# Hash attention and a gated block: the sums of a pair moved half a pair later, and for late pairs put beside the hash products of the next

## The chip, the cores and the metric

The kernel runs on one core of a Trainium2 chip. Times are device microseconds (us) of one launch; the kernel before was run three times. One further execution was recorded by the profiler. TensorE (PE) multiplies matrices into PSUM, ScalarE (ACT) applies functions, VectorE (DVE) does elementwise work, GpSimd (POOL) and SyncE (SP) here mainly issue DMAs. [...]

## What is computed

Attention in which a query sees only the keys of its own hash bucket, and then a gated feed-forward block on the result:

```python
q_bits = (np.einsum('bhsd,dk->bhsk', q, proj) > 0)      # 6 bits per token, k likewise
mask = q_bucket[:, :, :, None] == k_bucket[:, :, None, :]
scores = np.where(mask, scale * q @ k.T, -1e9)
attn = softmax(scores)                                   # over keys
x = (attn @ v)                                           # to (B*S, H*D)
g = x @ w_gate
out = (silu(g) * (x @ w_val)) @ w_out
```

There are 4 batches, 8 heads, 768 tokens and 64 channels a head; the block has 3072 tokens, width 512 and inner width 1536. The weights arrive as 8-byte numbers and are split on the chip into float32 parts ("words", "stage").

## The kernel before

The attention stage works on 16 pairs of heads (4 in each batch, NP = 4), and each pair n has two halves of 384 query tokens ("rows" of the work in the change's name). A half runs in three steps, written out by hand in the loop at lines 535 to 570; the order of that code is the order of each engine's queue.

First come six chunks of scores (`score`, 433): for both heads a float32 product of q and k and a bf16 product of hash bits into two PSUM banks, and then two exponentials on ScalarE (446) into the ring of A tiles. `add` (470) sums the A tiles of the half on VectorE (475, 479), one instruction per chunk from the second on, into `acc`, of which there are three. Last come six chunks of value products (`attend`, 449), which accumulate in the single av bank; at their end ScalarE copies av to xT (468), and in half 0 it also writes the small tile e (467), allocated at 466 from the pool `small`, which has two buffers per name.

All other PSUM tiles (scores, sums, hash, transposes) come in turn from one pool of seven banks (235), so that a tile waits until the last reader of the tile seven places before it is done.

Around this, the loop does three pieces of side work:

- **The sums.** `total` (484) multiplies the two acc tiles of a finished pair by a tile of ones (490, a 128x32 stationary operand, four column tiles side by side), ScalarE copies the result to row (493), and a small DMA on SP fetches few (495). `invert` (498) takes reciprocals on VectorE (499), writes them to DRAM (501) and reads them back spread over partitions as r (508, two DMAs). `norm` (512) multiplies xT by r on VectorE (514). For the pairs of the first batch it is followed by `split` (ScalarE 215, VectorE 218 and 222), for the others by a store to DRAM (519).
- **The next pair's operands.** `front` (350) returns steps. Up to pair 4 q and k are transposed by TensorE (356) and copied by ScalarE (359). From pair 5 on ("late") VectorE transposes blocks (410) that eight DMAs have fetched (268). Then `hash_next` multiplies by the hash matrix (369, also 128x32), ScalarE takes the signs of q at once (374), SP copies them to the other partitions (386, qb<-qb), and the rest, the signs of k and their spread on VectorE (383), is kept in the list `rest`, which the loop finishes after the scores.
- **The weights.** `scale_ahead` puts work on ScalarE (132, 124, 125), `prepare_on` on VectorE (150 to 166) and stores on POOL (168, with the loads of 117).

In pair n before the change: half 0 puts the sums of pair n-1 after its second chunk of scores, then the transposes of pair n+1, then `invert`; half 1 puts the hash products of pair n+1 after its third chunk, then the eight raw loads of pair n+2, the rest of the hash after the scores, and norm of pair n-1.

Of the kernel before, what the change touches and what calls it, by code (L numbers as in the profile page):

```python
# [19 lines left out]
def kernel(  # L20
# [29 lines left out]
    NP = H // 2  # L50
# [30 lines left out]
    def finish(todo):  # L81
        while todo:
            todo.pop(0)()
# [12 lines left out]
    n = 0  # L96
# [37 lines left out]
    def scale_ahead():  # L134
        if unrounded:
            round_up()
        i = progress["scaled"]
        if i < NPIECE and i < progress["kept"] + 3 and i in words:
            scale(i)
# [34 lines left out]
    def prepare_on(n):  # L174
        for _ in range(n):
            next(preparing, None)
# [17 lines left out]
    def bring(count=1):  # L194
        for _ in range(count):
            i = len(held)
            if i == len(wanted):
                return
            what, n = wanted[i]
            at = place[what, n % NF]  # L200
            while progress["kept"] <= at:
                next(preparing)
            held[what, n] = t = ringp.tile([P, 3, PIECE], FP32R, tag="ring", name="ring")
            nc.gpsimd.dma_start(t.bitcast(FP32), ram[at].bitcast(FP32))  # L204
# [23 lines left out]
    def attention(scope):  # L228
# [8 lines left out]
        def bank(name):  # L237
            return banks.tile([P, 512], FP32, tag="ps", name=name)
# [34 lines left out]
        def load(n, names):  # L273
            if n < len(pairs):
                for name in names:
                    fetch(n, name, nc.sync)
# [151 lines left out]
        waiting = []  # L428
# [4 lines left out]
        def score(u):  # L433
            n, half, c = units[u]
            qs = slice(half * HQ, (half + 1) * HQ)
            ks = slice(c * P, (c + 1) * P)
            sc = [bank("sc")[:, 0:HQ] for _ in range(2)]
            for x, start in ((T, True), (bits, False)):
                if u < 2 and not start:
                    prepare_pair(1)  # L440
                for h in range(2):
                    rows = slice(h * D, (h + 1) * D)
                    nc.tensor.matmul(sc[h], x["k", n][rows, ks], x["q", n][rows, qs],  # L443
                                     start=start, stop=not start)
            for h in range(2):
                nc.scalar.activation(weights(u)[:, h, 0:HQ], sc[h], AF.Exp,  # L446
                                     scale=SCALE * (OFF / 2 if n <= NP else 1.0))

        def attend(u):
            n, half, c = units[u]  # L450
            a = weights(u)
            if c == 0:
                av[n] = av_ps.tile([P, 512], FP32, tag="av", name="av")
            ps = av[n]
            width = AW if half == 0 else HQ
            for h in range(2):
                nc.tensor.matmul(ps[h * D : (h + 1) * D, 0:width], raws["v", n][:, h, c, :],  # L457
                                 a[:, h, 0:width], start=c == 0, stop=c == NCH - 1)
            if c == NCH - 1:
                if half == 0:  # L460
                    if n == len(pairs) - 1:
                        t = odd_x[NP - 1].tile([P, 3, S], FP32, tag=f"x{NP - 1}", name="lastx")
                        xT[n], spread[n] = t[:, 0], t[:, 1]
                    else:
                        xT[n] = xp.tile([P, S], FP32, tag="xT", name="xT")
                    mean[n] = small.tile([P, 1], FP32, tag="e", name="e")
                    nc.scalar.activation(mean[n], ps[:, HQ : HQ + 1], AF.Copy, scale=EPS)
                nc.scalar.copy(xT[n][:, half * HQ : (half + 1) * HQ], ps[:, 0:HQ])

        def add(u):  # L470
            n, half, c = units[u]
            a = weights(u)
            if c == 1:
                acc[n, half] = att.tile([P, 2, HQ], FP32, tag="acc", name="acc", bufs=3)
                nc.vector.scalar_tensor_tensor(out=acc[n, half], in0=weights(u - 1)[:, :, 0:HQ],
                                               scalar=S * EPS / P, in1=a[:, :, 0:HQ],
                                               op0=ALU.add, op1=ALU.add)
            elif c > 1:
                nc.vector.tensor_tensor(acc[n, half], acc[n, half], a[:, :, 0:HQ], op=ALU.add)  # L479
# [4 lines left out]
        def total(n):  # L484
            ps = bank("sum")
            t = [acc.pop((n, half)) for half in range(2)]
            for h in range(2):
                for half in range(2):
                    g = (2 * h + half) * BLOCK
                    nc.tensor.matmul(ps[g : g + BLOCK, 0:HQ], ones, t[half][:, h, :],  # L490
                                     start=True, stop=True)
            row = att.tile([P, HQ], FP32, tag="row", name="row", bufs=1)
            nc.scalar.copy(row, ps[:, 0:HQ])
            few = small.tile([P, each], FP32, tag="few", name="few")
            nc.sync.dma_start(few, row.rearrange("(g r) t -> r g t", r=BLOCK)[0])
            waiting.append(lambda: invert(n, few))

        def invert(n, few):
            nc.vector.reciprocal(few, few)
            s = sums[n % 2]  # L500
            nc.sync.dma_start(s, few)
            if n == len(pairs) - 1:
                t = spread[n].rearrange("p (x q) -> p x q", x=2)
            else:
                t = att.tile([P, 2, HQ], FP32, tag="r", name="r")
            flat = s.rearrange("p e -> (p e)").rearrange("(h x t) -> h (x t)", h=2, t=HQ)
            for h in range(2):
                nc.sync.dma_start(t[h * D : (h + 1) * D].rearrange("p x t -> p (x t)"),
                                  flat[h : h + 1].to_broadcast([D, 2 * HQ]))
            return lambda: norm(n, t)  # L510
# [13 lines left out]
        rest = []  # L524

        def prepare_pair(count):
            for _ in range(count):
                if steps:
                    rest.extend(f for f in steps.pop(0)() or [] if f)
# [4 lines left out]
        last = []  # L534
        for u in range(0, N, NCH):
            n, half, _ = units[u]
            more = n + 1 < len(pairs)
            for c in range(NCH):
                score(u + c)
                if u + c == 2 or more and half == 1 and c == 2:  # L540
                    prepare_pair(1)
                if half == 1 and c == 2:
                    load(n + 2, "qk")
                if c == 1 and half == 0 and n > 0:
                    total(n - 1)
                if c:
                    add(u + c)
            finish(rest)
            if half == 0 and more:
                steps = front(n + 1)  # L550
                if u:
                    prepare_pair(2)
            if half == 0:
                while waiting:
                    last.append(waiting.pop(0)())
            else:
                finish(last)
            for _ in range(1 if u else 2):
                scale_ahead()
            for c in range(NCH):  # L560
                attend(u + c)
            scale_ahead()
            if half == 1:
                load(n + 2, "v")
            elif more:
                if n + 1 <= NP:
                    prepare_pair(2 if u else 4)
            prepare_on(5 if 0 < n < NP else 4)
            if u >= N - 7 * NCH:
                bring()  # L570
# [5 lines left out]
    with ExitStack() as scope:  # L576
        attention(scope)
# [190 lines left out]
```

## Time and profile before

| | |
|---|---|
| median of 3 runs | 991.44 us (988.75 to 995.03) |
| profiled execution | 989.91 us, span on the core 988.0 us |
| mean granted TensorE clock | 0.981 |
| TensorE matmul busy | 952.0 us, 96% |
| weight loads / VectorE / ScalarE / GpSimd busy | 723.8 / 672.4 / 473.2 / 124.9 us |
| attention stage | 0 to 358 us; the gated block takes the rest |

A page of the profile gives, for each group of instructions, its source line, engine, operation, output and inputs, how many there are, the busy time and mean duration, and the idle time of the engine just before them with what ended it. A timeline lists the same instructions in order of time: start, duration, engine, line, operation, tiles, count, and in brackets the idle time before them and its releaser. Durations overlap where an engine is pipelined, so the distance between starts is what an instruction costs its queue. In the attention stage 2 to 4 such matmuls run side by side.

### The profile page before, as it was taken

Reading aid. Unit: us, or ns where it says so; the run is one execution under the profiler, and the core shown is the slowest. Engines: PE = TensorE matmul, PEld = TensorE weight load, DVE = VectorE, ACT = ScalarE, POOL = GpSimd, SP = SyncE. Lnnn points to the kernel's source line nnn. Section 1 sums busy time; section 2 is a strip of 40 time slices with the busy share of each in tenths; the row PEclk is TensorE's granted clock in tenths of the full one; section 3 lists DMA queues with packets and bytes.
Section 4 is the critical chain, followed back from the end, with each engine's and each line's share of the span. In section 5 each row is a group of like instructions: output and inputs, shape, how many; then the busy total and the mean of one; then the engine's idle time right before and its main releaser. Section 6 shows DMA issues by size and latency. Waiting matters only on the chain.

```text
span 988.0 us, 14458 instructions
## 1 busy us (share of the span) xinstructions
PE 952.0 (96%) x5413; PEld 723.8 (73%) x5413; DVE 672.4 (68%) x868; ACT 473.2 (48%) x882; POOL 124.9 (13%) x248
## 2 busy tenths in 40 slices
PE   9999989999999798788999999999999999999998
PEld 4444434444434368687999999999999999999997
DVE  4788988889877665647886446586546586546556
ACT  6899777887867553333422332322332322232221
POOL 3110010100111012011210110110110110110100
PEclk9999999999999898889999999999999999999999
DMA  6566677788888676485775854655854655754641
GB/s 181 169 184 186 151 175 202 194 210 202 200 207 261 183 264 239 161 298 197 300 280 181 312 191 142 232 207 185 310 189 156 226 205 192 255 189 163 224 160 65
DMA packets 134262, 203.22 MB, mean 206 GB/s; under 512 B 92912, under 2 KB 98512, under 8 KB 134192
## 3 DMA queue, kind: packets, MB, share of 16 engines
q0 software_dynamic: 31008, 159.79, 46.0%
q1 hardware_dynamic: 102384, 42.30, 17.7%
q8 instruction: 43, 0.70, 0.3%
q10 hardware_dynamic: 800, 0.20, 0.1%
q14 instruction: 27, 0.22, 0.1%
HBM read 162.01 MB, written 39.42 MB: 204 GB/s over the span
## 4 chain that ended last, share of the span: by engine, by line
PE 78%; DMA 6%; issue 6%; ACT 4%; DVE 3%; SPq 2%; ACTq 0%; DVEq 0%; POOLq 0%
PE a L597 23%; PE o L597 17%; PE sc L443 13%; PE n L597 12%; PE av L457 10%; DMA qb<-qb 3%; DMA ram<-stage 2%; SPq L268 2%; ACT A L446 2%; PE sum L490 1%; PE hps L369 1%; PE tps L356 1%; DVE o L689 1%; ACT qb L374 1%; DVE acc L479 1%
## 5 line engine op out<-in xcount | busy, mean ns | idle before, releaser
L597 PE MATMUL a<-xparts,ring 128*128 128x384 f32 x1536 | 286.5, 338 | 4.6 <-ACT g L639 3.2
L597 PEld LDWEIGHTS a<-xparts,ring 128*128 128x128 f32 x1536 | 272.0, 190 | 7.4 <-ACT g L639 3.6
L597 PE MATMUL o<-ring,hid 128*128 128x512 f32 x864 | 204.4, 397 | 8.9 <-ACT v L639 5.9
L597 PEld LDWEIGHTS o<-ring,hid 128*128 128x128 f32 x864 | 165.0, 192 | 44.5 <-ACT v L639 6.3
L446 ACT ACTIVATE A<-sc 128x384 f32<-128x384 f32 x384 | 157.7, 510 | 23.3 <-PE sc L443 22.9
L443 PE MATMUL sc<-qT,kT 64*128 64x384 f32 x768 | 166.5, 507 | 0.2 <-ACT A L446 0.2
L597 PE MATMUL n<-xparts,ring 128*128 128x384 f32 x768 | 150.1, 337 | 3.1 <-DVE o L689 3.1
L597 PEld LDWEIGHTS n<-xparts,ring 128*128 128x128 f32 x768 | 135.8, 190 | 3.4 <-DVE o L689 3.4
L479 DVE TENSOR_TENSOR acc<-acc,A 128x768 f32<-128x768 f32 x128 | 122.7, 958 | 22.0 <-ACT A L446 10.2
L645 DVE TENSOR_TENSOR v<-v,n 128x768 f32<-128x768 f32 x48 | 45.8, 954 | 128.4 <-PE n L597 101.7
L457 PE MATMUL av<-A,vraw 128*64 128x386 f32 (+1 forms) x768 | 131.2, 491 | 0.0
L204 POOL DMA_DIRECT2D ring<-ram x144 | 75.9, 529 | 436.8 <-PE n L597 282.5
L443 PEld LDWEIGHTS sc<-qT,kT 64*128 64x128 f32 x768 | 69.5, 189 | 73.0 <-issue 53.7
L457 PEld LDWEIGHTS av<-A,vraw 128*64 128x64 f32 x768 | 52.3, 136 | 71.8 <-issue 59.7
L639 ACT ACTIVATE g<-a 128x768 f32<-128x768 f32 x48 | 38.9, 811 | 126.6 <-PE a L597 126.6
L650 ACT ACTIVATE hid<-v 128x768 fp32r<-128x768 f32 x48 | 40.7, 847 | 115.9 <-DVE v L649 115.9
L689 DVE TENSOR_TENSOR o<-o 128x512 f32<-128x512 f32 x96 | 65.8, 687 | 27.7 <-ACT o L684 25.2
L647 ACT ACTIVATE g<-g 128x768 f32<-128x768 f32 x48 | 40.6, 847 | 87.8 <-DVE g L645 87.8
L443 PE MATMUL sc<-qb,kb 64*128 64x384 bf16 x384 | 69.7, 326 | 7.2 <-DMA qb<-qb 5.8
L645 DVE TENSOR_TENSOR g<-g,n 128x768 f32<-128x768 f32 x48 | 45.6, 949 | 37.8 <-PE n L597 29.7
L168 POOL DMA_DIRECT2D ram<-stage x36 | 19.7, 547 | 379.3 <-ACT A L446 165.2
L653 DVE SCALAR_TENSOR_TENSOR hid<-hid,v 128x768 fp32r<-128x768 f32 x48 | 45.9, 956 | 31.1 <-ACT hid L650 31.1
(77 smaller groups left out, 712.2 us busy)
## 6 DMA issues: line engine op xcount, KB each, us to landing
ring<-ram POOLq DMA_DIRECT2D x144, 768.0 KB, 5.6
ram<-stage POOLq DMA_DIRECT2D x36, 768.0 KB, 4.6
vraw<-in_v_dram SPq DMA_DIRECT2D x16, 384.0 KB
words<-in_moe_w_out_dram POOLq DMA_DIRECT2D x12, 512.0 KB, 7.1
out_dram<-o SPq DMA_DIRECT2D x24, 256.0 KB
r<-sums SPq DMA_DIRECT2D x30, 192.0 KB
words<-in_moe_w_gate_dram POOLq DMA_DIRECT2D x11, 512.0 KB, 7.4
words<-in_moe_w_val_dram POOLq DMA_DIRECT2D x11, 512.0 KB, 7.7
```

Source lines behind the costliest of these rows:

```text
L204: nc.gpsimd.dma_start(t.bitcast(FP32), ram[at].bitcast(FP32))
L443: nc.tensor.matmul(sc[h], x["k", n][rows, ks], x["q", n][rows, qs], start=start, stop=not start)
L446: nc.scalar.activation(weights(u)[:, h, 0:HQ], sc[h], AF.Exp, scale=SCALE * (OFF / 2 if n <= NP else 1.0))
L457: nc.tensor.matmul(ps[h * D : (h + 1) * D, 0:width], raws["v", n][:, h, c, :], a[:, h, 0:width], start=c == 0, stop=c == NCH - 1)
L479: nc.vector.tensor_tensor(acc[n, half], acc[n, half], a[:, :, 0:HQ], op=ALU.add)
L597: nc.tensor.matmul(ps, w, x, start=start, stop=stop)
L639: nc.scalar.activation(two(z), ops[what][2], AF.Copy, scale=STEP + 1)
L645: nc.vector.tensor_tensor(two(z), two(z), n_, op=ALU.subtract)
L647: nc.scalar.activation(z, z, AF.Silu)
L650: nc.scalar.activation(h, val, AF.Copy, scale=TOWARD / STEP)
L653: nc.vector.scalar_tensor_tensor(out=l, in0=h.bitcast(FP32), scalar=-STEP, in1=val, op0=ALU.mult, op1=ALU.add)
L689: nc.vector.tensor_tensor(accs[c], accs[c], t[:, 1], op=ALU.subtract)
```

## The change

The sums of pair n-1 move from the second chunk of half 0 of pair n to the start of half 1, right behind the value products of half 0, for n from 1 to 14; in the last pair they stay. Where pair n+1 is late (n from 4 on), its hash products are issued right behind those sums, ahead of the first scores of half 1, and the rest of the hash is finished after the second chunk of scores. `invert` moves from half 0 to half 1, after its scores, and `norm` from half 1 to half 0 of the following pair, after its transposes. The raw loads keep their place in the loop. The functions called are the same.

```diff
@@ -535,13 +535,21 @@
             n, half, _ = units[u]
             more = n + 1 < len(pairs)
+            final = not more
+            late = n + 1 > NP
+            if half == 1 and n > 0 and not final:
+                total(n - 1)
+            if half == 1 and more and late:
+                prepare_pair(1)
             for c in range(NCH):
                 score(u + c)
-                if u + c == 2 or more and half == 1 and c == 2:
+                if u + c == 2 or more and half == 1 and c == 2 and not late:
                     prepare_pair(1)
+                if half == 1 and c == 1 and late:
+                    finish(rest)
                 if half == 1 and c == 2:
                     load(n + 2, "qk")
-                if c == 1 and half == 0 and n > 0:
+                if c == 1 and half == 0 and final:
                     total(n - 1)
                 if c:
                     add(u + c)
@@ -550,11 +558,13 @@
                 steps = front(n + 1)
                 if u:
                     prepare_pair(2)
-            if half == 0:
-                while waiting:
-                    last.append(waiting.pop(0)())
-            else:
-                finish(last)
+            if half == 1:
+                finish(last)
+            while waiting and (half == 1 or final):
+                last.append(waiting.pop(0)())
+            if half == 0:
+                finish(last[:-1] if final else last)
+                last[:] = last[-1:] if final else []
             for _ in range(1 if u else 2):
                 scale_ahead()
             for c in range(NCH):
```

## The prediction

> **What bounds the kernel now.** I read the page first. TensorE is busy 96% of the span, so what counts is what lengthens its queue. The change touches only the attention stage (0 to 358 us), so I then listed TensorE, ScalarE and VectorE there in order of time. This is pair 11, half 0 from 244.88 and half 1 from 255.11, on TensorE (start, us, engine, line, operation, tile):
>
> ```profile
> 246.86 0.85 PE L490 MATMUL sum<-acc,ones 128*32 128x384 f32 x8
> 247.64 0.92 PE L443 MATMUL sc<-qT,kT 64*128 64x384 f32 x4
> 251.07 4.11 PE L457 MATMUL av<-A,vraw 128*64 128x386 f32 x24
> 255.11 0.92 PE L443 MATMUL sc<-qT,kT 64*128 64x384 f32 x4
> 257.74 0.52 PE L369 MATMUL hps<-qT,hash 128*32 128x384 f32 x2
> 258.52 0.92 PE L443 MATMUL sc<-qT,kT 64*128 64x384 f32 x4
> 261.14 4.09 PE L457 MATMUL av<-A,vraw 128*64 128x384 f32 x24
> ```
>
> There is no gap in it: the pair lasts 20.1 us from sum to sum (246.86 to 266.98). A chunk of scores takes 0.81; a half with neither sums nor hash is 9.07 (348.12 to 357.19: scores 5.05, value products 4.02). A half with either is about 0.98 longer. Eight such matmuls, four at a time, fill 0.64; the other 0.34 are two changes of tile shape, 0.17 each.
>
> The eleven pairs 4 to 14 last from the sums at 98.99 to those at 339.87: 240.9 us. At 20.1 they would be 221.1, so 19.8 are stalls. The list of waits (total, times, longest) names them:
>
> ```profile
> PE sc L443 <- DMA qb<-qb: 5.8, 4, 2.7
> PE hps L369 <- DVE qT L410: 5.4, 2, 5.0
> DVE xT L514 <- DMA r<-sums: 5.2, 3, 2.9
> ACT e L467 <- PE av L457: 14.1, 10, 2.7
> ```
>
> The first two lines are TensorE's. With what follows them (lost clock, the signs' spread) the waits on qb make about 10 of the 19.8; the late raw load of the last pair makes 7.35 (27.46 between sums at 312.41 and 339.87). The last line says that ScalarE is now ahead when it reaches line 467.
>
> The cost of an idle TensorE is in the clock, by stretches of 2 us (length, then busy times, clock, DMA share, GB/s):
>
> ```profile
> 286.00:288.00 2.00, 0.52 (x3) 0.12 (x2) 1.00 (x2) 0.49 (x1) 0.00 (x0) 1.00 1.38 164
> 288.00:290.00 2.00, 1.75 (x11) 0.71 (x14) 1.97 (x4) 0.63 (x2) 0.00 (x0) 0.69 0.78 116
> 290.00:292.00 2.00, 2.00 (x10) 0.51 (x4) 1.66 (x3) 1.21 (x3) 1.78 (x3) 0.50 0.92 173
> ```
>
> 1.73 us of idleness (0.27 and 1.46) was followed by half clock from about 288.75 to 292.16, which cost 1.6 us. Yet 2.71 us at 140.64 to 143.35 cost none. Stepping back from 288.75 by 43 windows of 3.413 us (the figure of the clock page named below), a boundary falls at 141.99 and cuts that gap into 1.35 and 1.36 (1.55 with a 0.20 before it): so between 1.55 and 1.73 idle in one stretch of 3.41 halves the next one.
>
> **The Trainium skill.** "TensorEngine Tiling (Array Packing)", Key Properties: a change of tiling mode drains TensorE; the trace agrees, 0.17 us each. "TensorE: Matmul & The Clock Gate", Part 1: the clock is halved by a monitor with free-running windows of about 3.4 us, after an idle window; the trace agrees on length and phase, but half an idle window was enough. The same page, Architectural detail: ScalarE and VectorE are strict queues, only weight loads are pulled ahead; the lists here show no exception. "PSUM — Partial Sum Buffer", Specifications: eight banks of 2 KiB. This kernel keeps one for av, and seven rotate.
>
> **The change, part by part.** The counts of instructions stay. ScalarE as it runs now in half 1 of pair 11, and VectorE in the last half of pair 15, which has neither sums nor hash:
>
> ```profile
> 255.26 0.17 ACT L467 ACTIVATE e<-av 128x1 f32<-128x1 f32 x1 [1.54 <-PE av L457]
> 255.32 0.47 ACT L468 COPY xT<-av 128x384 f32<-128x384 f32 x1
> 256.28 2.45 ACT L446 ACTIVATE A<-sc 128x384 f32<-128x384 f32 x6 [0.49 <-PE sc L443]
> 258.66 1.16 ACT L374 ACTIVATE qb<-hps,columns 32x384 bf16<-32x384 f32 x2
> 262.27 1.18 ACT L374 ACTIVATE kb<-hps,columns 32x384 bf16<-32x384 f32 x2
> ...
> 351.00 0.96 DVE L475 SCALAR_TENSOR_TENSOR acc<-A 128x768 f32<-128x768 f32 x1 [0.79 <-ACT A L446]
> 352.06 4.14 DVE L479 TENSOR_TENSOR acc<-acc,A 128x768 f32<-128x768 f32 x4
> ```
>
> (1) *TensorE's own work.* Half 0 loses the sums: 9.07. Half 1 has both products in one shape: 9.07 + 1.28 + 0.17 = 10.5. Together 19.6 against 20.1: three changes fewer, 0.5 us saved per late pair, if nothing waits. For pairs 1 to 3 only sums move, one change fewer: under 0.5 us in all; I take zero.
>
> (2) *The bank of the hash.* Seven banks rotate. Half 1 now takes sum, hash, two each for chunks 0 and 1, one for chunk 2; its second goes into sum's bank, and chunk 3 into the hash's bank, which is free only after the two k signs. These stand on ScalarE after chunk 1's exponentials. Before, the hash's bank was next wanted in the following half.
>
> (3) *A wait that moves to ScalarE.* Tile e (line 466, two buffers) is written at the end of half 0 of pair n and reuses the buffer of pair n-2. Its reader is norm, line 514. Before, norm(n-2) ran in half 1 of n-1, long past. Now it runs in half 0 of pair n, on VectorE behind the adds and both transposes. So line 467 waits for it, and behind 467 stand the copies of xT and row, all signs and exponentials of half 1.
>
> Times from the start of the sums in half 1 (t = 0), pairs 6 to 14. VectorE in half 0: adds end 8.0 after its start (348.12 to 356.13, above), transposes 0.89 and 0.94 (253.72, 254.62), norm 1.0: 10.8, which is t = 1.75. The second transpose ends at 0.77, so hash starts at 0.8, not 0.65, and scores at 1.6. ScalarE: e 1.8, xT 1.86, row 2.25, q signs 2.65 and 3.2, then four exponentials of 0.405 to 5.4, k signs of 0.58 to 6.6. TensorE has finished chunk 2 at 4.3 and stands until 6.65: **2.35 us idle**. Then three chunks 2.45 and value products 4.02: half 1 takes 13.1, the pair 13.1 + 9.07 = 22.2, **+2.1 each, 19 for nine pairs**.
>
> Pairs 4 and 5 are worse. Their half 0 normalises pairs 2 and 3, whose split (line 215, ScalarE) follows norm and stands ahead of the weight work (132, 124, 125) and of e. From norm at 10.8: 0.75, then 0.5 + 0.6 + 0.65, e and xT 0.45: row ends its slot at 14.1, t = 5.1 instead of 2.65. Half 1 becomes 15.5, the pair 24.6: +4.5; ScalarE enters pair 4 late from the transposing pairs, about 1.6, and stage work may add as much: I take **13 for both** (9 to 16).
>
> (4) *Clock.* An interval of 2.35 puts 1.65 or more into one 3.41 window for (3.41 - 2.35 + 2 x 0.70)/3.41 = 72% of phases. Loss 1.6 at full overlap; I take 1.2 on average: 9 x 0.72 x 1.2 = 8, and 2 x 1.6 = 3 for pairs 4 and 5, idle over 4: **+11** (0 to 17).
>
> (5) *What is regained.* q signs finish at 3.8 and the DMA of qb is wanted at 14: ten us instead of six (issue 303.87, wanted at 309.9), and r<-sums no longer stands ahead of it on SP. Its longest landing was 7.3, so these stalls go (10). k spread on VectorE also ends before half 0. The eight raw loads follow qb, start some 1.5 us earlier within a longer pair, and are wanted 1.8 earlier: the 7.35 goes mostly. Regained: **19.8** (10 to 19.8).
>
> (6) *SP and POOL.* SP's order becomes few, qb, eight loads, sums, two r, v, xram. r is issued after the loads (5.5 to 17 us of issue) near t = 15.5 and wanted at t = 22.9: 7.4 us, as now (258.26, wanted 265.3). But a late r now stops norm, and so ScalarE, and so TensorE: 0 to 10 us; I take zero, as a rival holds it. v has a whole pair of slack; POOL's order is unchanged. The reciprocal comes later and no longer waits for few (7.7 us of VectorE), hidden behind the adds' own pace.
>
> Sum: 19 + 13 + 11 - 19.8 = +23, less 0.5 for the early pairs: **+22**. Against the profiled execution, 989.91 us, that is 1012; this execution lies 1.5 below the median of 991.44. I keep 1012.
>
> **Rivals.**
> - *Clock holds* (22%): without (4), +11: 1002. For: 2.71 us passed once without loss. Against: the gaps recur at all phases.
> - *r comes late* (19%): three waits of 1.7 in the trace become TensorE's, doubled by loads ahead of them: +10, 1022.
> - *The other side: norm is not late* (13%). If norm ended before t = 0.15, or e's buffer was free otherwise, ScalarE would start row at 0.92 and the k signs would end at 5.8: idle 1.5, below the clock's limit, pair 21.4, eleven pairs 235.4, and 2 of stalls left: 237.4 against 240.9, 986. The point is whether VectorE reaches norm 1.6 us sooner; the adds' pace in the trace speaks against it.
> - *Banks do not bind* (4%): k signs done by 4.3. Pair 19.6, 216 in all, 5 left of the load stall: -20, 970. Against: from 0.9 ScalarE has 0.4 + 1.17 + 1.62 + 1.17 before it, 5.3 at best. This is also the case in which the change does what its words say.
>
> **The numbers.** The forecast itself has 42%. 1% of the median (981.5 to 1001.4) is what a measurement can tell from no change. Faster: the last rival and an edge of the third, 0.05. Within: most of the third and nearly half of the first, 0.21. Slower: 0.74. Range 990 to 1028: it leaves out the last rival, most of the third, and a late r with every clock window lost.
>
> **What would show it.** Gaps of about 2.3 us ahead of the fourth score chunk of half 1, ended by ScalarE's kb sign; line 467 ended by VectorE's 514 in pairs 6 to 14; the waits of PE on qb<-qb gone; granted clock below 1 in the slices from 110 to 340 us; pairs of 22 to 24 us, pairs 4 and 5 longest. I am wrong if chunk 3 follows chunk 2 without a gap, or if VectorE's norm ends before the value products of half 0.

## The result and the profile after

The changed kernel takes 1020.37 us (median of 4 runs, 1017.17 to 1024.35) against 991.24 us for the kernel before in the same comparison: a ratio of 1.0292, 95% interval 1.0242 to 1.0343. Its profiled execution has a span of 1019.5 us, 31.5 more than before, at a mean granted clock of 0.975.

The gated block is not where the time went: from its first product to the end of the span it takes 629.9 us (389.58 to 1019.5), before 629.4 (358.64 to 988.0). The attention stage is 30.9 us longer. TensorE's rows in the page of the kernel after (engine totals, then groups: busy time, mean ns, idle time before them and what ended most of it):

```profile
PE 968.9 (95%) x5413; PEld 737.9 (72%) x5413; DVE 672.5 (66%) x868; ACT 470.4 (46%) x882; POOL 124.9 (12%) x248
...
L443 PE MATMUL sc<-qT,kT 64*128 64x384 f32 x768 | 187.5, 527 | 14.1 <-ACT row L493 7.7
...
L443 PE MATMUL sc<-qb,kb 64*128 64x384 bf16 x384 | 83.4, 336 | 0.6 <-DVE kb L383 0.5
```

The wait of the scores on the DMA of qb is gone (0.6 us of idle time ahead of the second row, none of it the DMA). In its place the first row waits for ScalarE's copy of the row of sums. The list of waits between 90 and 395 us says what ScalarE waits for (engine, line, releaser: total us, times, longest):

```profile
ACT e L467 <- DVE xT L514: 39.7, 7, 10.1
...
DVE kb L383 <- ACT kb L374: 26.5, 11, 2.7
...
DVE xT L514 <- DMA r<-sums: 14.3, 7, 3.0
...
PE hps L369 <- DVE qT L410: 8.0, 2, 7.3
PE sc L443 <- ACT row L493: 7.7, 7, 2.3
```

The first line is the largest change: ScalarE stands at the small tile e until VectorE's norm has read the older one. Before, the same instruction waited only for TensorE's value products. In three more pairs the trace names the hash as the releaser of 467, which doesn't read it; in the one shown below norm ends at 254.65, as the hash does, and e begins at 254.74. So this list has only part of it.

Halves, from the first value product to the next half's first value product, in us ("half 1" of pair n, then half 0 of pair n+1):

| pair | before | after |
|---|---|---|
| 3 | 10.88, 10.36 | 15.61, 9.16 |
| 4 | 10.07, 10.99 | 17.38, 9.06 |
| 5 | 10.60, 13.44 | 15.10, 9.07 |
| 6 | 10.08, 10.05 | 13.71, 9.06 |
| 7, 10, 12 | 10.06 to 10.07, 10.21 to 13.84 | 12.10 to 12.15, 9.06 to 9.07 |
| 8, 9, 11, 13 | 10.07, 10.05 to 11.45 | 14.86 to 15.93, 9.06 to 9.07 |
| 14 | 17.41, 10.05 | 21.81, 10.05 |

Half 0 shrank by one microsecond as it had to; half 1 grew by 2 to 7. Pair 10 is an undisturbed one. TensorE in its half 1 (start, us, engine, line, operation, tiles, count):

```profile
253.00 0.85 PE L490 MATMUL sum<-acc,ones 128*32 128x384 f32 x8
253.81 0.52 PE L369 MATMUL hps<-qT,hash 128*32 128x384 f32 x2
...
257.26 0.97 PE L443 MATMUL sc<-qT,kT 64*128 64x384 f32 x3
...
259.60 1.10 PE L443 MATMUL sc<-qT,kT 64*128 64x384 f32 x3
...
261.11 4.09 PE L457 MATMUL av<-A,vraw 128*64 128x384 f32 x24
```

and ScalarE beside it:

```profile
254.74 0.17 ACT L467 ACTIVATE e<-av 128x1 f32<-128x1 f32 x1 [3.15 <-PE hps L369]
254.81 0.47 ACT L468 COPY xT<-av 128x384 f32<-128x384 f32 x1
255.17 0.50 ACT L493 COPY row<-sum 128x384 f32<-128x384 f32 x1
255.54 1.15 ACT L374 ACTIVATE qb<-hps,columns 32x384 bf16<-32x384 f32 x2
256.72 1.64 ACT L446 ACTIVATE A<-sc 128x384 f32<-128x384 f32 x4
258.38 1.16 ACT L374 ACTIVATE kb<-hps,columns 32x384 bf16<-32x384 f32 x2
```

A chunk takes 0.81, and chunk 2 starts at 256.31, so chunk 3 (257.26) is 0.14 late, right behind the first exponential (256.72 to 257.21): by its start it was given a bank that an exponential frees. The last chunk (259.60) begins 0.06 after the k signs end (259.54), and in v2, v3 and v5 below too it begins 0.04 to 0.05 after them (183.76 after 183.72 in v3): it is taken to be the one in the hash's bank. The half lasts 12.1 us.

Pair 8 is a disturbed one. VectorE's norm there comes late, because r has not landed:

```profile
204.88 0.94 DVE L410 STREAM_TRANSPOSE qT<-qraw 128x768 f32<-128x768 f32 x1
207.64 1.02 DVE L514 SCALAR_TENSOR_TENSOR xT<-xT,e,r 128x768 f32<-128x768 f32 x1 [1.83 <-DMA r<-sums]
```

ScalarE waits for it, with everything of half 1 behind:

```profile
208.76 0.17 ACT L467 ACTIVATE e<-av 128x1 f32<-128x1 f32 x1 [4.96 <-DVE xT L514]
```

TensorE then runs out of banks twice:

```profile
209.74 0.59 PE L443 MATMUL sc<-qT,kT 64*128 64x384 f32 x1 [0.56 <-ACT row L493]
...
211.27 1.31 PE L443 MATMUL sc<-qT,kT 64*128 64x384 f32 x3 [0.47 <-ACT A L446]
```

and the clock follows, in stretches of 2 us (length, busy times of PE, PEld, DVE, ACT, POOL, granted clock, DMA share, GB/s):

```profile
208.00:210.00 2.00, 1.44 (x10) 0.61 (x5) 1.97 (x4) 1.24 (x4) 0.00 (x0) 1.00 0.23 94
210.00:212.00 2.00, 1.53 (x7) 0.76 (x7) 0.93 (x2) 1.96 (x6) 0.86 (x2) 0.94 0.31 109
212.00:214.00 2.00, 2.00 (x10) 1.50 (x9) 0.41 (x1) 1.94 (x5) 0.20 (x1) 0.50 1.01 313
```

One late landing of 1.83 us so makes half 1 14.94 us long instead of 12.1. Norm waits for r (1.43 to 3.04 us) in pairs 6, 8, 9, 11 and 13, the five long ones, and the clock falls to half in three of them (8, 9 and 13).

### The profile page after: what moved, and what is told of

It is laid out like the page before. It is cut to its first block, busy times and chain, and to the rows that moved or that the text cites. A ratio compares the mean times of both kernels' runs of the same rounds, so it can differ in the third digit from the quotient of the medians.

```text
span 1019.5 us, 14489 instructions
## 1 busy us (share of the span) xinstructions
PE 968.9 (95%) x5413; PEld 737.9 (72%) x5413; DVE 672.5 (66%) x868; ACT 470.4 (46%) x882; POOL 124.9 (12%) x248
## 4 chain that ended last, share of the span: by engine, by line
PE 50%; issue 5%; DMA 3%; DVE 2%; ACT 1%; ACTq 0%; POOLq 0%
PE a L607 22%; PE o L607 16%; PE n L607 11%; DMA ram<-stage 3%; DVE o L699 1%; DVE o L696 0%; ACT words L125 0%; ACT stage L124 0%; DVE v L655 0%; DVE hid L663 0%; ACT g L657 0%; ACT v L649 0%; DVE v L659 0%; DVE stage L152 0%; ACT L657 0%
## 5 line engine op out<-in xcount | busy, mean ns | idle before, releaser
L607 PE MATMUL o<-ring,hid 128*128 128x512 f32 x864 | 202.3, 393 | 10.1 <-ACT v L649 5.9
L443 PE MATMUL sc<-qT,kT 64*128 64x384 f32 x768 | 187.5, 527 | 14.1 <-ACT row L493 7.7
L607 PEld LDWEIGHTS o<-ring,hid 128*128 128x128 f32 x864 | 162.7, 189 | 45.8 <-ACT v L649 6.4
L446 ACT ACTIVATE A<-sc 128x384 f32<-128x384 f32 x384 | 155.1, 510 | 9.1 <-PE sc L443 8.5
L443 PEld LDWEIGHTS sc<-qT,kT 64*128 64x128 f32 x768 | 87.3, 198 | 84.2 <-issue 44.2
L443 PE MATMUL sc<-qb,kb 64*128 64x384 bf16 x384 | 83.4, 336 | 0.6 <-DVE kb L383 0.5
L655 DVE TENSOR_TENSOR g<-g,n 128x768 f32<-128x768 f32 x48 | 45.6, 950 | 37.3 <-PE n L607 29.4
```

Source lines behind the costliest of these rows:

```text
L607: nc.tensor.matmul(ps, w, x, start=start, stop=stop)
L655: nc.vector.tensor_tensor(two(z), two(z), n_, op=ALU.subtract)
```

## The experiments

Each kernel below was timed in alternation with the kernel before (990.75 to 992.19 us beside them). Ratios are to that, with the 95% interval.

| kernel | us | ratio |
|---|---|---|
| the change | 1020.4 | 1.0292 (1.0242 to 1.0343) |
| v1: e in four buffers | 1008.5 | 1.0192 (1.0167 to 1.0218) |
| v2: v1, norm in half 1 | 998.5 | 1.0082 (1.0060 to 1.0104) |
| v3: only the hash moved | 1001.7 | 1.0125 (1.0097 to 1.0153) |
| v4: only the sums moved | 1014.7 | 1.0251 (1.0222 to 1.0280) |
| v5: v2, spread later | 995.3 | 1.0038 (1.0015 to 1.0061) |
| v6: v5, norm first | 1000.2 | 1.0087 (1.0043 to 1.0132) |
| v7: v3, spread later | 1002.6 | 1.0112 (1.0087 to 1.0138) |
| v8: v2, hash back in its place | 981.5 | 0.9906 (0.9863 to 0.9950) |
| v9: v6, k signs late again | 988.6 | 0.9975 (0.9961 to 0.9989) |
| v10: v8, hash behind chunk 0 | 982.7 | 0.9918 (0.9888 to 0.9948) |
| v12: the change, k signs late again | 1017.7 | 1.0271 (1.0228 to 1.0313) |
| v13: v9, early hash from pair 6 on | 986.2 | 0.9948 (0.9933 to 0.9963) |

**First question: is it the wait of e, and which half of the change makes it?** The theory was that the reuse of e carries the delay of norm to ScalarE. v1 is the change with

```diff
-                    mean[n] = small.tile([P, 1], FP32, tag="e", name="e")
+                    mean[n] = small.tile([P, 1], FP32, tag="e", name="e", bufs=4)
```

> The changed kernel with four buffers for the tile e instead of two. My theory: line 467's wait for norm (39.7 us of ScalarE in seven waits) is what makes half 1 of pairs 6 to 13 last 12.1 to 15.9 us; without it row is copied near 0.9 us after the sums start, the k signs end near 5.8, and half 1 lasts 10.5 to 10.8. That takes 25 to 28 us off: 1020 becomes 992 to 996. Pairs 4 and 5 (17.4 and 15.1) stay long, because line 215 still waits for norm. Rival, the bank of the hash alone binds: half 1 stays at 12 us or more in pairs 6 to 13 and the time stays above 1008.

Measured 1008.5: 12 us gone, half of what the theory wanted, and neither account holds: the time is on the rival's side of 1008, the halves are not. Line 467 no longer waits for norm, and half 1 of the undisturbed pairs 6, 8, 9 and 11 falls to 11.34 to 11.52 us, not to 10.8. Pairs 4 and 5 stay long (20.44 and 15.30), and VectorE still stands when r is late, with the adds behind norm. That is now VectorE's longest wait:

```profile
DVE xT L514 <- DMA r<-sums: 24.3, 9, 5.6
```

v2 puts norm back into half 1, now of the pair after, where r has had a whole pair:

```diff
-            if half == 0:
+            if half == 0 and final:
                 finish(last[:-1] if final else last)
```

> As the run with four buffers of e, and norm moved from half 0 back to half 1, one half later than in the changed kernel, so that it stands behind the adds of half 1 and r has a whole pair to land. My theory: line 215 no longer waits in half 0, half 1 of pairs 3, 4 and 5 falls from 15.6, 17.4 and 15.1 to about 11, 10.7 and 10.7, and pairs 6 to 13 stay at 10.5 to 10.8: 974 to 982, faster than the kernel before (991). Rival, moving sums and hash costs by itself, whatever norm does: 995 or more.

Measured 998.5: another 10 us, and the rival's range held. With both waits off ScalarE the kernel is still slower than before. v3 and v4 split the change. v3 is the kernel before with these lines alone (`late` as in the change):

```diff
+            if half == 1 and more and late:
+                prepare_pair(1)
...
-                if u + c == 2 or more and half == 1 and c == 2:
+                if u + c == 2 or more and half == 1 and c == 2 and not late:
                     prepare_pair(1)
+                if half == 1 and c == 1 and late:
+                    finish(rest)
```

> The kernel before with the hash products of late pairs alone moved ahead of the first scores of half 1; sums, reciprocals and norm stay where they were. My theory: the waits on qb<-qb go (about 10 us with what follows them), no long gap appears, since line 467 waits for nothing new, and the second transpose delays the hash by about 0.5 us a pair: 980 to 988. Rival, the hash's bank binds: each late pair 1 to 2 us longer, 995 to 1005.

v4 is the change without the moved hash:

```diff
-            late = n + 1 > NP
+            late = False
```

> The changed kernel with the hash products left behind the third chunk of scores in all pairs; sums, reciprocals and norm stand where the change puts them. My theory: line 467 still waits for norm, and behind a late r, so half 1 is long in the same pairs, but the hash's bank no longer adds to it: 1000 to 1012. Rival, the hash's place causes the loss: 991 or below.

Both missed, each on the slow side: the hash alone costs 10.9 us against the kernel before in the same runs (990.8), the sums alone 23.9, together 29.1: less than the sum of both. v3 lies in its rival's range. In its trace half 1 of pair 7 is 1.0 us longer than before: 0.47 is a wait of the hash for the second transpose, and the last chunk, which follows the k signs by 0.04, takes 0.6 more than before (183.76 to 185.28, 1.52 instead of 0.91). Pairs 4, 5 and 14 together are 7 us longer than before. In v4 the wait on norm is larger than in the change itself:

```profile
ACT e L467 <- DVE xT L514: 51.3, 9, 11.4
```

So e and norm belong to the moved sums. The early hash has a cost of its own, which v1 and v2 don't touch.

**Second question: what does the early hash cost?** In v2 an undisturbed pair lasts 21.13 to 21.26 us (pair 11 from value product to value product: 261.52 to 282.65). TensorE's own share, as foretold, would be 19.6, but it waits for VectorE's transpose (0.67 of idle time ahead of the hash at 267.08). VectorE around it:

```profile
266.09 0.93 DVE L410 STREAM_TRANSPOSE qT<-qraw 128x768 f32<-128x768 f32 x1
...
272.05 0.85 DVE L383 TENSOR_SCALAR kb<-kb,columns 32x768 bf16<-32x768 bf16 x2 [2.40 <-ACT kb L374]
272.83 0.94 DVE L475 SCALAR_TENSOR_TENSOR acc<-A 128x768 f32<-128x768 f32 x1
273.87 4.15 DVE L479 TENSOR_TENSOR acc<-acc,A 128x768 f32<-128x768 f32 x4
277.94 1.01 DVE L514 SCALAR_TENSOR_TENSOR xT<-xT,e,r 128x768 f32<-128x768 f32 x1
...
287.35 0.94 DVE L410 STREAM_TRANSPOSE qT<-qraw 128x768 f32<-128x768 f32 x1
```

This reads as a loop, a circle of steps of which each needs the one before it or stands behind it in its queue: transposes, hash (TensorE), q signs, exponentials, k signs (ScalarE), spread, adds, norm, the adds of half 0, transposes (VectorE). Nothing in it is slow, but it is 21.1 us long, and VectorE stands 2.40 us in it. v5 cuts it where the wait stands, by issuing the spread behind the adds of chunks 1 to 3:

```diff
-                if half == 1 and c == 1 and late:
-                    finish(rest)
+                if half == 1 and c == 1 and late and more:
+                    finish([rest.pop(0), rest.pop(0)])
+                if half == 1 and c == 4 and late:
+                    finish(rest)
```

> The run with four e buffers and norm in half 1, and in the late pairs the VectorE step that spreads the k signs (L383) issued behind the adds of chunks 1 to 3 instead of ahead of all adds; the two sign operations on ScalarE stay where they are. Theory A, a loop through VectorE and ScalarE of 21.1 us a pair (the spread stands ahead of the adds and waits for the signs, the transposes stand behind the adds, the next signs behind the transposes): the wait of L383 on ACT kb (30.8 us there) falls under 5 us, the hash's wait on DVE qT goes in most late pairs, a pair lasts 19.6 to 20.2 us, and the kernel takes 983 to 990 us. Theory B, the 21.1 us come from something else (the banks of chunks 3 to 5, ScalarE's order): a pair stays at 21 us and the kernel at 994 to 1001 us.

Theory A fell in this form: 995.3 us is in the rival's range, and an undisturbed pair still takes 21.02 us. VectorE in v5 shows why:

```profile
205.07 0.96 DVE L475 SCALAR_TENSOR_TENSOR acc<-A 128x768 f32<-128x768 f32 x1 [1.59 <-ACT A L446]
207.16 2.02 DVE L479 TENSOR_TENSOR acc<-acc,A 128x768 f32<-128x768 f32 x2 [1.13 <-ACT A L446]
```

The 2.40 us did not go; they are now 1.59 + 1.13 of waiting for exponentials, which stand on ScalarE behind the q signs and behind the k signs. On this reading the loop was not cut, since it also runs through the exponentials. v7 makes the same edit to v3:

> The run that moved only the hash of the late pairs (sums in half 0 as before), and in it the spread of the k signs behind the adds of chunks 1 to 3. Theory A: the wait of L383 on ACT kb (26.1 us there) goes, half 1 goes from 11.1 to about 10.1 us, some 9 us less: 990 to 995 us. Theory B: half 1 stays at 11.1 us because the hash's own products and its bank make it longer: 998 to 1004 us.

1002.6, and half 1 11.03 instead of 11.08 to 11.13 us: the place of the spread decides nothing there either. v6 takes work out of the loop instead, norm into the time in which VectorE waits anyway:

```diff
+            if half == 1 and n > NP:
+                finish(last)
             if half == 1 and n > 0 and not final:
                 total(n - 1)
```

> The run before it in this list, and in the late pairs norm (VectorE, 0.93 us) issued ahead of everything in half 1 instead of behind its scores. Theory A: norm fills time in which VectorE would wait, so the adds of half 0 end 0.9 us earlier; where VectorE still sets the pair this gives another 0 to 8 us, 977 to 988 us. Theory B: the copy of xT that norm reads ends late, so norm waits at the head of VectorE and the adds behind it with it: 990 to 1000 us.

The pairs do what theory A says: half 1 of pairs 6 to 13 is 11.32 to 11.36 us, with no wait for the transposes left, and a pair 20.4. The time does not: 1000.2 us, over a wide spread (994.28 to 1005.24). In the trace, which is of the shortest of its runs, half 1 of pairs 4 and 5 takes 14.59 and 17.38 us, and the last pair gives more back. Its sums run in half 0, so r comes late for a norm at the head of half 1: norm waits 2.60 us for r there, the reciprocal 3.59 for few just before, the adds stand behind both, and the last sums wait 5.26 for them. The trace cannot show why the median is 5 us above v5's: the profiled executions of the two differ by 0.4 us.

What is left of half 1, 11.35 against 10.57 of TensorE's own work, was ascribed to the k signs ahead of the exponentials. v9 is v6 with the early finish taken out and norm first only where another pair follows:

```diff
-                if half == 1 and c == 1 and late and more:
-                    finish([rest.pop(0), rest.pop(0)])
-                if half == 1 and c == 4 and late:
-                    finish(rest)
...
-            if half == 1 and n > NP:
+            if half == 1 and n > NP and more:
```

> The run with four e buffers, norm first in half 1 (not in the last pair, where it waited for r) and the hash ahead of the second row's scores, but the k signs where the kernel before has them, behind all exponentials of half 1, and their spread behind all adds. Theory A, what is left of the cost of the early hash is the two k sign operations ahead of the exponentials of chunks 2 to 5 (half 1 lasts 11.35 us with them, of which TensorE's own work is 10.57): half 1 goes to 10.6 us, a pair to 19.7 us, and the kernel takes 971 to 979 us, less than the run that left the hash in its place (981.5). Theory B, the hash's bank is then held through half 1 and the scores of chunks 3 to 5 wait for banks: half 1 stays at 11.2 us or more, 983 to 990 us.

The pairs do what A says, the kernel does not: half 1 of pairs 7 to 13 is 10.58 to 10.76 and a pair 19.74 us, the shortest of all, but 988.6 us is in theory B's range. TensorE in half 1 of pair 8 stands nowhere:

```profile
198.11 0.85 PE L490 MATMUL sum<-acc,ones 128*32 128x384 f32 x8
198.92 0.52 PE L369 MATMUL hps<-qT,hash 128*32 128x384 f32 x2
...
199.70 0.92 PE L443 MATMUL sc<-qT,kT 64*128 64x384 f32 x4
...
204.75 4.09 PE L457 MATMUL av<-A,vraw 128*64 128x384 f32 x24
```

The gain is lost at the edges of the stage. In pairs 4 and 5 half 1 takes 14.39 and 16.75 us, since the hash waits 1.98 and 2.76 for the transposes: VectorE has the split of xT (lines 218 and 222, and a wait on ScalarE) in those pairs. In pair 14 norm waits for r with all adds behind it:

```profile
326.80 1.02 DVE L514 SCALAR_TENSOR_TENSOR xT<-xT,e,r 128x768 f32<-128x768 f32 x1 [3.27 <-DMA r<-sums]
```

**Third question: what are the moved sums worth, with their two waits taken away?** v8 is v2 with `late = False`.

> The run that moved only the sums (the hash of the late pairs where it was), with four e buffers and norm in half 1. Theory A: what moving the sums cost came from norm and e; with both off the path a pair lasts as before or 0.5 us less, 984 to 992 us. Theory B: the sums in half 1 cost by themselves (row ahead of the exponentials on ScalarE, the products' wait for the last add): 996 to 1008 us.

981.5 us, faster than the kernel before, by 0.5 to 1.4%. Against v2 the only difference is the place of the hash and of the signs that come with it: it is worth 17 us there (12 between the profiled executions; v8's was the slowest of its four, 987.4). Against v4 the difference is the four buffers of e and the place of norm: 33 us. The steps from the change to v1, v2 and v8 so give 12, 10 and 17 us. In v8's pair 8, on TensorE and VectorE:

```profile
195.11 0.85 PE L490 MATMUL sum<-acc,ones 128*32 128x384 f32 x8
195.90 0.92 PE L443 MATMUL sc<-qT,kT 64*128 64x384 f32 x4
...
198.52 0.52 PE L369 MATMUL hps<-qT,hash 128*32 128x384 f32 x2
```

```profile
194.93 0.94 DVE L410 STREAM_TRANSPOSE qT<-qraw 128x768 f32<-128x768 f32 x1
```

The hash starts 2.6 us after the sums' slot ends, when the second transpose has been done since 195.87, and the signs of k stay behind the exponentials. An undisturbed pair is 10.85 + 9.07 = 19.92 us. v10 moves the hash halfway, behind chunk 0:

```diff
-                if u + c == 2 or more and half == 1 and c == 2 and not late:
+                if u + c == 2 or more and half == 1 and c == (0 if n + 1 > NP else 2):
```

> The run that moved only the sums, with four e buffers and norm in half 1 (981.5), and in it the late pairs' hash behind the scores of chunk 0 of half 1 instead of chunk 2; the k signs stay behind the exponentials. Theory A, an earlier hash is harmless as long as the k signs stay late, and takes away the waits on the DMA of qb (0.72 and 2.12 us there): a pair 19.9 us, 976 to 981 us. Theory B, the hash's bank is held two chunks longer and the scores wait for banks, or the transposes are not done in time: 984 to 992 us.

982.7: between the two ranges, and not to be told from v8. Pairs 7 to 13 have 10.85 to 10.86 in half 1, so a hash behind chunk 0 with late k signs costs an undisturbed pair nothing. But pairs 4 to 6 wait for the transposes (0.97, 1.77 and 0.65 us), and one wait on qb stays (4.04 us in pair 13). v13 is v9 with the early hash and early norm only from pair 6 on:

```diff
-            late = n + 1 > NP
-            if half == 1 and n > NP and more:
+            late = n + 1 > NP + 2
+            if half == 1 and n > NP + 1 and more:
```

> The run with late k signs (988.6), and in it the early hash and the early norm only from half 1 of pair 6 on; in half 1 of pairs 4 and 5, where norm is followed by the split of xT into xparts (two more VectorE steps and a wait on ScalarE, 2.9 us), the hash stays behind chunk 2. Theory A: the early hash lost its gain in pairs 4 and 5, where the hash waited 1.98 and 2.76 us for the transposes (14.39 and 16.75 us of half 1, against 12.16 and 11.14 in the run that left the hash in its place): these go back to 12.2 and 11.2 us, the later pairs stay at 19.7 us, and the kernel takes 976 to 983 us. Theory B: the loss comes from somewhere else (the waits on qb, the last pair): 985 to 990 us.

986.2 us: in theory B's range, 2.4 below v9. Pair 5 went back to 11.08 us, pair 4 did not (15.36; its hash now waits 2.75 for ScalarE's row), and the last pairs still stand behind norm and the reciprocal. In the profiled executions v8, v9 and v13 end the attention stage within 0.4 us of each other (356.71, 356.30, 356.39), and v8's is of its slowest execution; so what separates v8 from v9 in the medians (7 us, disjoint intervals) isn't in these traces, and stays open.

**Is it the early k signs in the change as made?** v12 undoes them alone:

```diff
-                if half == 1 and c == 1 and late:
-                    finish(rest)
```

> The changed kernel with one edit undone: the k signs and their spread stand behind all scores and adds of half 1 again, as before the change. Theory A: the early signs and spread cost 1.5 to 2.5 us a late pair by themselves, but the wait of e on norm (39.7 us in 7 waits) stays: 1000 to 1010 us. Theory B: the wait on norm sets the pairs alone, and the edit only moves time into it: 1015 to 1021 us.

1017.7, an interval that overlaps the change's own: theory B held. The early signs do cost something by themselves: half 1 of pairs 7, 10 and 12 is 11.24 to 11.42 us here, 12.1 in the change. But other halves are longer (pair 6 16.92 instead of 13.71, pair 4 19.23 instead of 17.38), e still waits for norm (37.3 us in 7 waits), and of the difference the time keeps less than these runs can tell.

## Why the prediction was right, and where its sum was wrong

The side and the place were right, and 1012 us is 8 below the median; the rival with the late r (1022) came closer. The terms are not the ones that were measured, and one of the signs by which the prediction said it would be wrong came true: chunk 3 follows chunk 2 with next to no gap (0.14 us). The stage by its rows, in us:

| | before | after | difference | forecast |
|---|---|---|---|---|
| pairs 6 to 14, nine undisturbed | 181.1 | 190.5 | +9.4 | +19, and 8 of clock |
| late r in five of them, with its clock | 0 | 14.2 | +14.2 | 0 |
| the late raw load, pair 14 | 7.3 | 10.7 | +3.4 | -7.3 |
| other stalls of pairs 6 to 14 | 7.0 | 0 | -7.0 | -7.0 |
| pairs 4 and 5 | 45.1 | 50.6 | +5.5 | +13, 3 of clock, -4.9 of stalls |

The undisturbed rows are nine times 20.12 and nine times 21.17 (12.1 + 9.07); the late r is what pairs 6, 8, 9, 11 and 13 have over 21.17 each. The 45.1 hold 4.9 of stalls over twice 20.12. Together +25.5; the prediction had +23. The first pairs add 3.0 and the last half and its sums 2.4, which makes 30.9.

(1) *TensorE's own work*: right. Half 0 is 9.06 to 9.07; half 1 without a stall 10.58 to 10.68 in v9, against 10.5. For the early pairs "I take zero" was 3 short: ahead of half 1 of pair 3 (15.61 us) ScalarE waits 4.35 us at line 215, the split of xT, for a norm that now comes late.

(2) *The bank of the hash*: this step failed. It put chunk 3 into the hash's bank, by a strict rotation of seven, as the section on the kernel before has it. By the starts in the trace the banks of this pool go out in the order in which they come free: chunk 3 follows a first exponential, and only the last chunk waits for the k signs. So the idle stretch of 2.35 us did not come. The half lasts 12.1, not 13.1, and a pair without further trouble keeps its clock.

(3) *The wait that moves to ScalarE*: right in mechanism and in time. From the start of the sums e begins at 1.74 (said: 1.8), row at 2.17 (2.25), the q signs at 2.54 (2.65), and the k signs end at 6.54 (6.6). v1, which takes only this wait away, is 12 us faster. Pairs 4 and 5 were foretold as the longest. Pair 4 (26.44 us) is passed only by pair 14 (31.86), but pair 5 (24.17) also by pairs 3, 11 and 13 (24.39 to 25.00). Their half 1 is 17.38 and 15.10 where 15.5 for each was the working, and the addition for stage work was too much.

(4) *The clock*: half clock came, but not behind the bank: in pairs 8, 9 and 13 it came behind the late r. The rule of the step, that 1.55 to 1.73 us of idleness in one stretch of 3.41 halve the next, doesn't hold in the trace after either: there 1.02 us were enough in one place, and 1.69 were not in another (last section).

(5) *What is regained*: the waits on qb went, as said. "The 7.35 goes mostly" failed: the raw loads of the last pair are issued behind qb and take 14.3 us of issue (327.07 to 341.41), and the hash, now wanted earlier, waits 7.33 for the transpose behind them (half 1 21.81):

```profile
352.94 0.86 PE L369 MATMUL hps<-qT,hash 128*32 128x384 f32 x2 [7.33 <-DVE qT L410]
```

v8, whose hash stands three chunks later, waits 2.99 there.

(6) *r*: "I take zero, as a rival holds it". This was the largest term left out. The rival priced it at 10 us; it was 14.2 in pairs 6 to 13, and more in pair 14. The chain was named: r late, norm late, ScalarE late, TensorE late. Between 90 and 395 us there are seven waits on r, 14.3 us in all, against three of 5.2 before. The loads ahead of r on SP are only part of the cause: in pairs 6, 9, 11 and 14 the write of the reciprocals is issued 0.9 to 6.1 us after they are ready, as soon as the loads are out, but in pairs 8 and 13 it goes out at once, and norm still begins only 8.6 and 9.7 us after r's issue. Why r lands late there is open; no run put r ahead of the loads with the sums in their new place.

So errors of opposite sign cancelled, and that the sum comes within 8 us of the median is luck in good part: the bank (with its clock) some 18 us too high, r and the raw load some 25 too low; pairs 4 and 5 were some 6 too high. The sum itself also takes 0.5 off for the early pairs, which step (1) had put at zero, and rounds 22.7 to 22.

What no step said: the early hash is dear even with e and norm out of the way (v2 against v8, 17 us). The reading is that it closes a loop through TensorE, ScalarE and VectorE that is longer than any engine's work. v2, v5, v6 and v9 are consistent with it, each by the pair's length (21.13 to 21.26, 21.02, 20.4, 19.74). That the loop is the whole of the 17 us isn't shown, since v9 has the shortest pairs and is not the fastest.

## What to carry to other kernels

When a step is moved between two engines' queues, follow the small tiles it writes: a buffer of one column, reused one pair too early, put VectorE's delay on ScalarE's head and cost 12 us, and four buffers removed it. A product that TensorE can do earlier is only worth moving if its inputs have slack there. Here the hash three chunks later cost TensorE 0.2 us a pair (v8 against v9) and spared the kernel 17 us where the k signs were early too (v2), 7 where they were late (v9). A short period in the middle of a stage says little about its edges: count the first and last pairs too.

## What the runs showed of the hardware beyond that

The clock was halved after less idleness than the kernel before had shown, and idle time alone doesn't sort the cases. The half clock of pair 8 begins at 211.76. The stretch of 3.41 us ahead of it and the one that begins there, then two from pair 11 on the same grid (20 stretches later; columns as above):

```profile
208.35:211.76 3.41, 2.39 (x13) 1.00 (x10) 2.54 (x5) 2.97 (x8) 0.62 (x2) 1.00 0.31 117
211.76:215.18 3.42, 3.42 (x15) 2.82 (x15) 1.55 (x3) 3.36 (x9) 0.44 (x1) 0.50 0.94 252
276.62:280.03 3.41, 1.72 (x12) 0.75 (x8) 1.98 (x3) 0.90 (x4) 0.00 (x0) 1.00 0.21 63
280.03:283.45 3.42, 2.88 (x15) 1.74 (x16) 1.63 (x3) 3.35 (x9) 1.21 (x2) 1.00 0.40 125
```

In pair 8 TensorE was idle for 1.02 us (0.56 and 0.47), and the next stretch ran at half clock. In pair 11 it was idle for 1.69, and the next ran at full clock, as the one after 1.55 did before. One difference is visible: between the two gaps of pair 8 the matmuls ran one or two at a time and not four, ahead of the gap of pair 11 side by side as usual. Whether that is what counts, no run took apart.
